# Attention and two MoE layers on one core: conversions of the first weights moved from three steps to the two behind them

## The chip, the cores and the metric

One Trainium2 chip, one of its cores. The metric is the device time of the kernel in microseconds (us), from one launch of the whole program. Lower is better.

## What is computed

The reference chains three layers over 4 batches of 576 tokens:

```python
scores = np.where(causal, -1e9, q @ k.T / 8 + cum_i - cum_j)     # 8 heads of 64
attn = softmax(scores) @ v                                       # -> x, 2304 x 512
h = np.maximum(np.maximum(x @ w1, x @ w2), x @ w3)               # 512 -> 768
x2 = h @ w_out                                                   # 768 -> 512
h = x2 @ w_in                                                    # 512 -> 2048
g = (a0 + a1*h + a2*h**2 + a3*h**3) / (1 + abs(b0)*abs(h) + abs(b1)*h**2 + 1e-6)
out = g @ w_out2                                                 # 2048 -> 512
```

All weights arrive as float64. The kernel converts them on the chip.

## The kernel before

**Stages.** Attention and the first MoE layer run interleaved (up to about 480 us of the profiled execution), the second MoE layer follows. A matrix product is made of three matmuls over parts called high and low: the value rounded for TensorE and what rounding left.

**Attention** goes by pairs of heads (class `Pair`, line 278) and by two groups of query rows: group 0 is rows 0 to 319, group 1 is rows 320 to 575. The first batch's eight pairs have one group each: pairs 0 to 3 do group 0, pairs 4 to 7 group 1. So the fourth pair, number 3, is the last one that group 0 of the first batch needs. A `Unit` (line 358) is one head of a pair's group, and there is one unit per step of the main loop (line 606). It is spread over three steps: in its own step the scores (TensorE, lines 388 to 391), masking and minimum (VectorE, line 392), the exponential (ScalarE, line 399) and the scaling by the row sums (GpSimd, line 412, or ScalarE, line 410); in the next step its transposes (line 432) and their copies (line 434); in the step after that, for every second unit, the product with v (`attend`, line 448), its high part x (ScalarE, line 455) and low part (VectorE, line 456). So the fourth pair's two units are those of steps 6 and 7, and its x is written in step 9.

**Idle matmuls.** For pairs 0 to 3, `exercised` (line 80) issues two matmuls of 512 columns on constant data ahead of each real group (line 84). Nothing reads them.

**First MoE layer.** `moe1_units` (line 517) gives 22 units for each batch and group: 18 of `moe1_h` (line 475, twelve matmuls on lines 482 to 484, one weight tile per unit, taken in the order in which tiles are converted) and four of `moe1_o` (line 499), which need all tiles of the second weights. The first 22 come into a queue in step 9. `fill` (line 565) is called six times a step; it pops conversions as `conv_due` (line 587) wants, and spreads the 22 units over the steps up to 24.

**Conversions.** There are 18 of 512 elements a partition (the first weights, `convert_w1`, line 214), then 12 of 256 (`convert_wo`, line 223). Each has four stages (`stages`, line 169): `magnitude` on ScalarE (line 181), `bits` as four instructions on VectorE (lines 186, 187, 188, 191), `high` on ScalarE (line 197), `low` on GpSimd (line 200). Raw weights are loaded by SyncE's queue (`load_raw`, line 163, 512 KB for each of the first 18) into six buffers, three ahead at the start and then two ahead of the conversion (`pipelined`, line 249). Two conversions are made before the loop. Then:

```python
def conv_due(step):
    state["c"] += 0.15 if step < 7 else 0.5
    return NCONV - int(state["c"])
```

which, at six calls a step, is 0.9 a step up to step 6 (eight conversions in all by then) and three a step from step 7 on, 30 by step 14.

**Order of the work.** The program is traced in this order, and the Tile scheduler then orders each engine's instructions: earlier in the program means higher priority, and an instruction of lower priority goes ahead when, by the scheduler's own model of time, nothing of higher priority is ready. Engines then execute in that fixed order. `tc.issue_after(ins)` keeps what its block traces behind `ins` on the engine of `ins`; on line 398 the exponentials of the first batch's units are so kept behind the last x. `keep_in_program_order` pins the order of the raw loads.

Of the kernel before, what the change touches and what calls it, by code (L numbers as in the profile page):

```python
# [8 lines left out]
F32 = mybir.dt.float32  # L9
F32R = mybir.dt.float32r  # L10
I32 = mybir.dt.int32
AF = mybir.ActivationFunctionType
# [25 lines left out]
def kernel(  # L38
    ctx: ExitStack, tc: tile.TileContext, q, k, v, f, w1, w2, w3, w_out, m2_in, m2_out, m2_a, m2_b, out
):  # L40
    nc = tc.nc
# [8 lines left out]
    NPAIR = H // 2  # L50
    NB = len(Q0)

    def r32(ap):
        return ap.bitcast(F32)
# [25 lines left out]
    def exercised(bank, n):  # L80

        if n < 4:
            for _ in range(WARM):
                nc.tensor.matmul(bank, warm[:, 0], wide, start=True, stop=True)
        return bank
# [36 lines left out]
    LOOK, WHOLE, PRE = 2, 6, 2  # L122
# [36 lines left out]
    E_LO, E_HI = 2.0**-15, float.fromhex("0x1.dffffep+16")  # L159

    raws = {}

    def load_raw(src, nm_):
        shape = list(src.shape)
        rp, rt, rb = (mpool, "x1", 8) if shape[1] * shape[2] <= 256 else (wpool, "x2", 6)
        raws[nm_] = rp.tile(shape[:-1] + [2 * shape[-1]], I32, name=f"raw_{nm_}", tag=rt, bufs=rb)
        tc.keep_in_program_order(nc.sync.dma_start(raws[nm_], src.bitcast(I32)))

    def stages(split, src, nm_, pool, tag, bufs, pin):
        shape = list(src.shape)  # L170
        at = {}

        def held(ins):
            return tc.keep_in_program_order(ins) if pin else ins

        def magnitude():
            raw = raws.pop(nm_)
            raw = raw.rearrange("p c (f t) -> p c f t", t=2)
            at["low"], at["top"] = raw[:, :, :, 0], raw[:, :, :, 1]
            at["t"] = pool.tile(shape, I32, name=f"cv_{nm_}", tag=tag, bufs=bufs)  # L180
            held(nc.scalar.activation(at["t"].bitcast(F32), at["top"].bitcast(F32), AF.Abs))

        def bits():
            t, low, top = at["t"], at["low"], at["top"]
            tf = t.bitcast(F32)
            held(nc.vector.tensor_scalar(tf, tf, E_LO, E_HI, op0=ALU.max, op1=ALU.min))
            nc.vector.tensor_scalar(t, t, 0x07FFFFFF, 3, op0=ALU.bitwise_and, op1=ALU.logical_shift_left)
            nc.vector.scalar_tensor_tensor(
                out=t, in0=low, scalar=29, in1=t, op0=ALU.logical_shift_right, op1=ALU.bitwise_or
            )  # L190
            nc.vector.scalar_tensor_tensor(
                out=t, in0=top, scalar=-0x40000000, in1=t, op0=ALU.bitwise_and, op1=ALU.bitwise_or
            )

        def high():
            at["hi"], at["lo"] = split()
            held(nc.scalar.activation(at["hi"], at["t"].bitcast(F32), AF.Copy))

        def low():
            held(nc.gpsimd.tensor_tensor(at["lo"], at["t"].bitcast(F32), r32(at["hi"]), op=ALU.subtract))  # L200

        return [magnitude, bits, high, low]

    def convert(hi, lo, src, nm_, pool, tag, bufs):
# [6 lines left out]
    def raw_w1(fc, j):  # L211
        return rows((w1, w2, w3)[j])[:, :, fc * P : (fc + 1) * P], f"w{j}_{fc}"

    def convert_w1(fc, j):
        if fc not in w1t:
            w1t[fc] = [wpool.tile([P, 3, NDC, P], F32R, name=f"w1{x}_{fc}", tag="w", bufs=12) for x in "hl"]
        hi, lo = (t[:, j] for t in w1t[fc])
        convert(hi, lo, *raw_w1(fc, j), mpool, "x1", 8)
# [30 lines left out]
    def pipelined(work, look, begun=False):  # L249

        n = len(work)

        def go(i):
            for j in range(0 if i == 0 and not begun else i + look + (i == 0), min(i + look + 1, n)):
                work[j][0]()
            work[i][1]()

        return [lambda i=i: go(i) for i in range(n)]
# [5 lines left out]
    def pinned(ld):  # L264
        tc.keep_in_program_order(ld)
# [92 lines left out]
    class Unit:  # L358
# [77 lines left out]
        def attend(self):  # L436

            p, h, g = self.pair, self.h, self.g
            if h == 0:
                return  # L440
            lo, hi = GQ[g]
            w = hi - lo
            ot = exercised(ps_o.tile([P, 512], F32, name=f"o_{self.nm}", tag="o"), p.n)
            order = list(GCH[g].items())
            with tc.high_priority():
                for j, (c, (col, q0)) in enumerate(order):
                    for i in (1, 0):
                        mm = nc.tensor.matmul(  # L448
                            ot[SIDES[i][0], q0 - lo : w], p.v[:, c, i], p.pt[g][:, i, col : col + hi - q0],
                            start=(j == 0), stop=(j == len(order) - 1),  # L450
                        )
                        if (j, i) != (0, 1):
                            pinned(mm)
            x = mpool.tile([P, 2, w], F32R, name=f"x_{self.nm}", tag=f"x{g}", bufs=(6, 8)[g])
            out_ = nc.scalar.activation(x[:, 0], ot[:, :w], AF.Copy)
            nc.vector.tensor_tensor(x[:, 1], ot[:, :w], r32(x[:, 0]), op=ALU.subtract)  # L456
            xt[p.b, p.hp, g] = x
            if p.b == 0:
                last["x"] = out_.ins


    hs = {}
# [54 lines left out]
    def moe1_units(b, g):  # L517
        return [lambda fc=fc, j=j: moe1_h(b, g, fc, j) for fc in range(NF1) for j in range(3)] + [
            lambda dc=dc: moe1_o(b, g, dc) for dc in range(NDC)
        ]  # L520
# [7 lines left out]
    conv = [  # L528
        (lambda fc=fc, j=j: load_raw(*raw_w1(fc, j)), lambda fc=fc, j=j: convert_w1(fc, j))
        for fc in range(NF1)  # L530
        for j in range(3)
    ]
# [2 lines left out]
        for fc in range(NF1)  # L535
        for z in range(2)
    ]
    ahead = [load_ for load_, _ in conv[: LOOK + 1]]
    conv = pipelined(conv, LOOK, True)
    wps = [(c, z) for c in range(NF2) for z in range(2)]  # L540
    conv2 = []
    for i, cz in enumerate(wps):
# [12 lines left out]
    for n, p in enumerate(pairs):  # L555
        if p.hp == NPAIR - 1:
            at = first.get(n + 1, len(slots)) + 1
# [4 lines left out]
    state = {"m": 0, "of": 1, "n": 0}  # L562
# [22 lines left out]
    state["c"] = state["c2"] = 0.0  # L585

    def conv_due(step):
        state["c"] += 0.15 if step < 7 else 0.5
        return NCONV - int(state["c"])

    pairs[0].load()
# [14 lines left out]
    for step in range(len(slots) + 2):  # L606
        u = slots[step] if step < len(slots) else None
        t = slots[step - 1] if 0 <= step - 1 < len(slots) else None
        o = slots[step - 2] if 0 <= step - 2 < len(slots) else None
        prep, NPRE = [], 0  # L610
        if u is not None and u.pair.n + 1 < len(pairs):
            n = u.pair.n + 1
            at = first[n] - (2 if len(pairs[n - 1].groups) == 2 else PRE if pairs[n].whole else 1)
            if step == at:
                prep = pairs[n].prepare()
                NPRE = pairs[n].ng + 1
        if o:
            o.attend()
            if step in ready:
                queue.append((step, [x for bg in ready[step] for x in moe1_units(*bg)]))  # L620
        if step == 16:
            pinned(nc.sync.dma_start(ab[:, 0:4], m2_a.partition_broadcast(P)))
            pinned(nc.sync.dma_start(ab[:, 4:6], m2_b.partition_broadcast(P)))
        fill(step)
        if t:
            t.turn(0)
        fill(step)
        if t:
            for bank in range(1, len(GBANK[t.g])):
                t.turn(bank)  # L630
        fill(step)
        for f_ in prep[:NPRE]:
            f_()
        if u:
            blks = GBLK[u.g]
            u.begin()
            for i in blks[:-1]:
                u.scores(i)
            fill(step)
            u.scores(blks[-1])  # L640
        else:
            fill(step)
        fill(step)
        for f_ in prep[NPRE:]:
            f_()
        fill(step)
        if u:
            u.normalise()
        for p in lvat.get(step, []):
            p.load_v()  # L650
        if prep and n + 1 < len(pairs):
            pairs[n + 1].load()
# [50 lines left out]
    a0, a1, a2, a3, b0, _, b1, one = (ab[:, i : i + 1] for i in range(8))  # L703
# [161 lines left out]
```

## Time and profile before

| | |
|---|---|
| median of 3 runs | 956.12 us (954.08 to 957.19) |
| the profiled execution's own time | 953.65 us |
| its span, first to last instruction | 951.6 us |
| TensorE's mean granted share of full clock | 0.996 |
| busy: TensorE, VectorE, ScalarE, GpSimd | 98%, 76%, 68%, 25% |
| chain that ended last: TensorE, VectorE, ScalarE, issue, DMA | 84%, 9%, 2%, 2%, 2% |

The busy share of TensorE counts modelled ends of matmuls that overlap in the pipeline; distances between starts tell more. The chain follows the last instruction back to what released each step, so its shares say which engine set the end.

### The profile page before, as it was taken

The page shows a single profiled execution, that of the slowest core. Times are in us where ns is not written, and L with a number is a line of the kernel's source. Part 1 is how long each engine was busy: PE and PEld are TensorE (multiplying, and loading weights), DVE is VectorE, ACT ScalarE, POOL GpSimd, SP SyncE. Part 2 cuts the span into 40 slices and gives each one's busy share as a digit, 9 for nine tenths or more (in the row PEclk, how much of TensorE's full clock was granted, in tenths as well). Part 3 has the DMA queues.
Part 4 walks back from the last instruction along what each step waited for, and adds up shares of the span by engine and source line. Part 5 has one row for each costly group of instructions (what it writes and reads, how often), then busy time and mean ns, then how long its engine had stood idle before and what let it go on. Part 6 is the DMA issues. An engine that isn't in the chain of part 4 may idle for free.

```text
span 951.6 us, 16833 instructions
## 1 busy us (share of the span) xinstructions
PE 930.5 (98%) x5780; PEld 825.3 (87%) x5780; DVE 723.0 (76%) x1692; ACT 648.8 (68%) x1542; POOL 241.3 (25%) x392
## 2 busy tenths in 40 slices
PE   6999999999999999999999999999999999999998
PEld 4758989988999989999999988888888888899997
DVE  8897854556776767534296969888888988899996
ACT  6898877767767676646354567667666766677765
POOL 4654424444555555414132300000000000000000
PEclk9989999999999999999999999999999999999999
DMA  7871431133556455220246386011002102100000
GB/s 192 227 229 52 111 106 45 44 87 102 149 151 194 124 159 165 65 79 2 68 145 192 118 296 235 1 45 45 0 1 70 42 1 67 44 1 1 34 1 34
DMA packets 125741, 88.52 MB, mean 93 GB/s; under 512 B 74572, under 2 KB 110424, under 8 KB 125656
## 3 DMA queue, kind: packets, MB, share of 16 engines
q1 hardware_dynamic: 125656, 87.45, 30.7%
q8 instruction: 46, 0.75, 0.3%
q14 instruction: 39, 0.32, 0.1%
HBM read 64.73 MB, written 22.69 MB: 92 GB/s over the span
## 4 chain that ended last, share of the span: by engine, by line
PE 84%; DVE 9%; ACT 2%; issue 2%; DMA 2%; SPq 1%; POOL 0%; ACTq 0%; DVEq 0%; POOLq 0%
PE hq L740 7%; PE oo L788 7%; PE hq L738 7%; PE hq L739 7%; PE oo L789 7%; PE oo L787 7%; PE h L482 6%; PE h L483 6%; PE h L484 6%; PE o L448 5%; PE tp L432 5%; PE x2p L508 2%; PE s L391 2%; PE s L390 2%; PE x2p L510 2%
## 5 line engine op out<-in xcount | busy, mean ns | idle before, releaser
L482 PE MATMUL h<-x,w1h 128*128 128x320 f32 (+1 forms) x576 | 175.7, 305 | 2.3 <-DVE x L456 2.0
L483 PE MATMUL h<-x,w1h 128*128 128x320 f32 (+1 forms) x576 | 172.2, 299 | 0.0
L484 PE MATMUL h<-x,w1l 128*128 128x320 f32 (+1 forms) x576 | 171.8, 299 | 0.0
L482 PEld LDWEIGHTS h<-x,w1h 128*128 128x128 f32 x576 | 109.2, 190 | 4.3 <-DVE x L456 2.3
L788 PE MATMUL oo<-wp,gh 128*128 128x512 f32 x288 | 112.7, 391 | 0.0
L399 ACT ACTIVATE e<-e,st 128x64 f32<-128x64 f32 (+4 forms) x160 | 89.0, 557 | 34.2 <-DVE st L392 33.0
L787 PE MATMUL oo<-wp,gh 128*128 128x512 f32 x288 | 112.1, 389 | 0.0
L747 ACT ACTIVATE s<-hq 128x512 f32<-128x512 f32 (+1 forms) x80 | 44.3, 554 | 97.6 <-PE hq L740 97.5
L483 PEld LDWEIGHTS h<-x,w1h 128*128 128x128 f32 x576 | 109.4, 190 | 0.4 <-issue 0.2
L484 PEld LDWEIGHTS h<-x,w1l 128*128 128x128 f32 x576 | 109.2, 190 | 0.0
L789 PE MATMUL oo<-wp,gl 128*128 128x512 f32 x288 | 109.2, 392 | 0.0
L412 POOL TENSOR_SCALAR e<-e,rs 128x64 f32<-128x64 f32 (+4 forms) x144 | 79.0, 563 | 103.3 <-DVE rs L406 87.8
L392 DVE CUSTOM_DVE_ANT_0 e<-s,mask 128x320 f32<-128x320 f32 (+3 forms) x160 | 67.0, 431 | 38.9 <-PE s L391 33.3
L750 DVE SCALAR_TENSOR_TENSOR s<-s,ab,u 128x512 f32<-128x512 f32 (+1 forms) x80 | 55.7, 697 | 32.3 <-ACT u L748 32.1
L434 ACT ACTIVATE pt<-tp 128x384 f32<-128x384 f32 (+3 forms) x160 | 69.4, 469 | 15.7 <-PE tp L432 14.0
L432 PE MATMUL tp<-ident,e 128*128 128x128 f32 (+1 forms) x480 | 75.8, 276 | 1.3 <-POOL e L412 0.9
L740 PE MATMUL hq<-x,wil 128*128 128x512 f32 (+1 forms) x192 | 69.9, 364 | 0.0
L738 PE MATMUL hq<-x,wih 128*128 128x512 f32 (+1 forms) x192 | 69.8, 364 | 0.0
L739 PE MATMUL hq<-x,wih 128*128 128x512 f32 (+1 forms) x192 | 69.7, 363 | 0.0
L789 PEld LDWEIGHTS oo<-wp,gl 128*128 128x128 f32 x288 | 54.1, 188 | 11.3
L787 PEld LDWEIGHTS oo<-wp,gh 128*128 128x128 f32 x288 | 54.1, 188 | 10.4
L788 PEld LDWEIGHTS oo<-wp,gh 128*128 128x128 f32 x288 | 54.1, 188 | 10.4
(133 smaller groups left out, 2433.3 us busy)
## 6 DMA issues: line engine op xcount, KB each, us to landing
raw_w<-in_moe_w_dram SPq DMA_DIRECT2D x18, 512.0 KB
raw_wp<-in_moe_w_out_dram SPq DMA_DIRECT2D x32, 256.0 KB
wpd<-wp SPq DMA_DIRECT2D x32, 256.0 KB
raw_wi<-in_moe_w_in_dram SPq DMA_DIRECT2D x32, 256.0 KB
wp<-wpd SPq DMA_DIRECT2D x10, 768.0 KB
x2d<-xo SPq DMA_DIRECT2D x16, 320.0 KB
out_dram<-ob SPq DMA_DIRECT2D x18, 256.0 KB
kn<-in_k_dram SPq DMA_DIRECT2D x32, 128.0 KB
```

What stands on the lines that cost most here:

```text
L399: nc.scalar.activation(e[:nr], e[:nr], AF.Exp, bias=m, scale=-1.0, accum_out=l)
L412: nc.gpsimd.tensor_scalar(e, e, self.rs[:, 1, j : j + 1], 0.0, op0=ALU.mult, op1=ALU.add)
L432: nc.tensor.transpose(tp[:kr, dst : dst + P], self.e[i][:, Q0[c] : Q1[c]], ident)
L482: nc.tensor.matmul(hp_[:, :w], wh[:, j, dc], xs[dc][:, 1], start=(dc == NDC - 1), stop=False)
L483: nc.tensor.matmul(hp_[:, :w], wh[:, j, dc], xs[dc][:, 0], start=False, stop=False)
L484: nc.tensor.matmul(hp_[:, :w], wl[:, j, dc], xs[dc][:, 0], start=False, stop=(dc == 0))
L738: nc.tensor.matmul(hp_[:, :w], wih[:, dc, fs], xh, start=(dc == 0), stop=False)
L739: nc.tensor.matmul(hp_[:, :w], wih[:, dc, fs], xl, start=False, stop=False)
L740: nc.tensor.matmul(hp_[:, :w], wil[:, dc, fs], xh, start=False, stop=(dc == NDC - 1))
L787: nc.tensor.matmul(o, g[0][:, ts_], wh_, start=(fc == 0), stop=False)
L788: nc.tensor.matmul(o, g[0][:, ts_], wl_, start=False, stop=False)
L789: nc.tensor.matmul(o, g[1][:, ts_], wh_, start=False, stop=(fc == NF2 - 1))
```

## The change

After the eighth conversion none is due in steps 7, 8 and 9. One raw load is issued at the head of each of these three steps instead. In steps 10 and 11 conversions come at one per `fill`, six a step, then three a step as before; the 30th falls in step 15. From the ninth on, raw weights are loaded five ahead instead of two. Every conversion traced from step 10 on has its first ScalarE instruction kept behind the fourth pair's x.

```diff
     raws = {}
+    fourth = {"x": None}
...
-            held(nc.scalar.activation(at["t"].bitcast(F32), at["top"].bitcast(F32), AF.Abs))
+            with tc.issue_after(fourth["x"]) if fourth["x"] else nullcontext():
+                held(nc.scalar.activation(at["t"].bitcast(F32), at["top"].bitcast(F32), AF.Abs))
...
                 last["x"] = out_.ins
+                fourth["x"] = fourth["x"] or (out_.ins if p.n == NPAIR - 1 else None)
...
-    ahead = [load_ for load_, _ in conv[: LOOK + 1]]
-    conv = pipelined(conv, LOOK, True)
+    loads = [load_ for load_, _ in conv]
+    ahead = [loads.pop(0) for _ in range(LOOK + 1)]
+
+    def convert_next(i, run):
+        while loads and NC - len(loads) < i + (LOOK if i < HELD else FAR) + 1:
+            loads.pop(0)()
+        run()
+
+    NC, HELD, FAR = len(conv), 8, 5
+    conv = [lambda i=i, run=run: convert_next(i, run) for i, (_, run) in enumerate(conv)]
...
-        state["c"] += 0.15 if step < 7 else 0.5
+        state["c"] += 0.15 if step < 7 else 0.0 if step < 10 else 1.0 if step < 12 else 0.5
...
+        if 7 <= step < 10:
+            loads.pop(0)()
         if o:
             o.attend()
```

## Rows read from the trace of the kernel before

**Rows 1.** Stretches: busy us of each engine (xcount), granted clock, DMA share, GB/s.
```profile
30.90:50.90 20.00, 20.00 (x121) 15.68 (x120) 16.12 (x44) 16.84 (x50) 10.53 (x13) 1.00 0.90 245
50.80:74.20 23.40, 19.23 (x86) 11.52 (x84) 23.40 (x53) 21.24 (x54) 13.70 (x13) 0.85 0.65 193
74.20:142.50 68.30, 67.30 (x483) 62.67 (x483) 47.48 (x145) 53.99 (x140) 26.96 (x41) 1.00 0.34 91
200.00:480.00 280.00, 277.75 (x2162) 258.36 (x2161) 170.52 (x555) 182.60 (x543) 125.80 (x222) 1.00 0.40 115
```
**Rows 2.** The chain that ended last, in order of time: start us, us, what.
```profile
41.81 1.34 PE o L448 x12
...
46.83 0.47 PE s L84 x2
47.30 0.54 PE s L388 x2
47.84 0.33 PE tp L432 x3
...
70.57 1.68 DVE cv_w L188
...
73.79 0.41 DVE x L456
...
142.47 2.17 PE o L448 x20
```
**Rows 3.** TensorE in order of time: start us, us, instruction, count, idle before.
```profile
61.23 1.02 PE L388 MATMUL s<-kf,qf 66*128 66x448 f32 x2 [1.18 <-DVE st L392]
...
66.40 2.62 PE L448 MATMUL o<-pt,v 128*64 128x320 f32 x12
...
74.24 0.42 PE L482 MATMUL h<-x,w1h 128*128 128x320 f32 x1 [2.04 <-DVE x L456]
...
76.10 0.31 PE L482 MATMUL h<-x,w1h 128*128 128x320 f32 x1
```
**Rows 4.** VectorE's groups, 50.8 to 74.3 us: busy us, mean ns, idle before.
```profile
L188 DVE SCALAR_TENSOR_TENSOR cv_w<-raw_w,cv_w 128x512 int32<-128x512 int32 x8 | 7.4, 927 | 0.0
...
L392 DVE CUSTOM_DVE_ANT_0 e<-s,mask 128x320 f32<-128x320 f32 (+3 forms) x7 | 3.2, 460 | 0.0
```
**Rows 5.** TensorE's groups, same stretch and columns.
```profile
L388 PE MATMUL s<-kf,qf 66*128 66x320 f32 (+2 forms) x18 | 8.2, 551 | 2.0 <-DVE st L392 2.0
L432 PE MATMUL tp<-ident,e 128*128 128x128 f32 (+1 forms) x21 | 4.2, 312 | 0.2
L448 PE MATMUL o<-pt,v 128*64 128x320 f32 (+2 forms) x24 | 4.0, 489 | 0.0
```
**Rows 6.** ScalarE's groups, same stretch and columns.
```profile
L197 ACT ACTIVATE w1h<-cv_w 128x512 fp32r<-128x512 f32 x7 | 4.4, 625 | 0.0
L181 ACT ACTIVATE cv_w<-raw_w 128x512 f32<-128x512 f32 x6 | 4.0, 666 | 0.0
```
**Rows 7.** VectorE's group of first weights left behind 74.3 us, to 142.5 us.
```profile
L191 DVE SCALAR_TENSOR_TENSOR cv_w<-raw_w,cv_w 128x512 int32<-128x512 int32 x1 | 0.7, 677 | 0.0
```
**Rows 8.** VectorE in order of time: start us, us, instruction.
```profile
63.76 1.38 DVE L187 TENSOR_SCALAR cv_w<-cv_w 128x512 int32<-128x512 int32 x1
65.06 1.49 DVE L186 TENSOR_SCALAR cv_w<-cv_w 128x512 f32<-128x512 f32 x1
...
67.48 0.41 DVE L186 TENSOR_SCALAR cv_w<-cv_w 128x512 f32<-128x512 f32 x1
```
**Rows 9.** GpSimd in order of time, same columns.
```profile
63.58 2.67 POOL L200 TENSOR_TENSOR w1l<-cv_w,w1h 128x512 fp32r<-128x512 f32 x2
```
**Rows 10.** SyncE's queue in order of time.
```profile
54.39 3.86 SPq L167 DMA_DIRECT2D raw_w<-in_moe_w_dram  x4
58.34 8.27 SPq L167 DMA_DIRECT2D raw_wo<-in_moe_w_out_dram  x4
69.06 0.38 SPq L269 DMA_DIRECT2D v<-in_v_dram  x1
```

## The prediction

> **What bounds the kernel now.** I first read busy time by stretches [rows 1]. From 200 to 480 us TensorE is busy for 277.75 of 280 us, so behind the start nothing but TensorE's own work sets the pace: what TensorE loses early is lost at the end, and what it gains early stays, unless it is lost again later. The stretch that is different is 50.8 to 74.2 us, steps 7 to 9. There VectorE is busy for all of its 23.4 us, TensorE's granted clock is 0.85 on average, and TensorE has 86 matmul records, where the 20 us before had 121 [rows 1].
>
> Next I read the chain [rows 2]. Up to about 50 us it runs over TensorE. Then it runs over VectorE's conversion lines, such as the 1.68 us piece of line 188 at 70.57, and it comes back to TensorE only through the fourth pair's low part of x (line 456 at 73.79). In TensorE's own order of time [rows 3] the same is seen from the other side: a score matmul waits 1.18 us for VectorE at 61.23, the fourth pair's product with v takes 2.62 us at 66.40, where the same twelve matmuls took 1.34 at 41.81 [rows 2], and the first matmul of the MoE layer starts at 74.24 after 2.04 us of waiting for x. The doubled time is the clock: a mean of 0.85 over the stretch [rows 1] is (1 - 0.85) x 23.4 / 0.5 = 7.0 us at the lower of two levels, 1.2 GHz instead of 2.4. What came before the fall was TensorE waiting for VectorE [rows 3].
>
> **What the change removes.** The unions of VectorE's time: of the 23.4 us, masking and minimum (lines 392), x and the reciprocals take about 6.3 us (the largest group, 3.2 us, in [rows 4]). The other 17.1 us are conversions of the first weights, about 7.5 of them (eight instructions of line 188 [rows 4], seven of others), so 2.3 us each. All of these leave the stretch. Eight conversions are allowed before the fourth pair's x, and the kernel before has, behind 74.3 us, only one last instruction of line 191 left of eighteen conversions [rows 7]. So some 9.3 conversions move behind x: the 7.5 of this stretch and about two that had been pulled ahead of it. The new order on ScalarE makes this certain, since VectorE's four instructions need line 181's result.
>
> What TensorE must do in the stretch, at full clock: 18 score matmuls at 0.54 / 2 = 0.27 us [rows 2, 5], 4.9 us; 21 transposes at 0.33 / 3 = 0.11, 2.3 us; 24 products with v at 1.34 / 12 = 0.11, 2.7 us. The other 23 of the 86 are idle matmuls (0.47 / 2 = 0.235 each [rows 2]) and transposes of keys and queries, about half each; at 0.17 they make 3.9 us. Together 13.8 us, so the stretch holds **23.4 - 13.8 = 9.6 us** that a free VectorE could give back, the clock's part included.
>
> Not all of it comes back. ScalarE's 21.24 us there [rows 1] lose 4.4 + 4.0 us of conversions [rows 6] and so about 12.8 remain, below TensorE's 13.8; but steps 8 and 9 hold scores without idle matmuls, and a chain of score, minimum, exponential and transpose has waits of its own. The row nearest is the 20 us before, where TensorE never sat idle beside 0.9 conversions a step [rows 1]: nothing lost. At the other end, the waits and the lower clock stay as they are in the last part, some 4 us. I take 1.1 us, nearer to the first, since VectorE, which ended those waits, is three quarters freed. First term: **-8.5 us** (-9.6 to -5.6).
>
> **What it adds behind x.** From 74.2 to 142.5 us, where pair 7's product with v starts [rows 2], whose x lets the next 22 units begin, VectorE is busy for 47.48 of 68.3 us and ScalarE for 53.99 [rows 1]. Into this come 9.3 conversions. On ScalarE they cost 0.625 + 0.666 = 1.29 us each [rows 6], 12.0 us against 14.3 idle. On VectorE at 2.3 us they cost 21.4 us against 20.8 idle. So both engines would be full, which no chain of dependent instructions reaches. What covers TensorE is the store of MoE units: twelve matmuls, 76.10 - 74.24 = 1.86 us each [rows 3]; the eight that have weights are 15 us of work, and a conversion each 2.3 us adds the next. What gives way is the attention of steps 10 to 17, whose masks queue on VectorE behind the conversions and whose transposes and products wait for them, and the last four units, for which the twelve second conversions are due one step later.
>
> Bounds of this second term: nothing, if the 12 second conversions slip behind pair 7's x and the units cover the rest; or +13 us, if the lost attention runs alone (rival D). A packing of about 94% fits the work of 47.5 + 21.4 = 68.9 us into 73 us, which against 68.3 is 5 us late, with part of it covered by units that run meanwhile. I take **+4 us**, between nothing and the full lateness, nearer to the latter.
>
> A GpSimd instruction beside a conversion can stretch it: lines 187 and 186 took 1.38 and 1.49 us while two subtractions of line 200 ran from 63.58 to 66.25, and 0.41 us at 67.48 alone [rows 8, 9]. My 2.3 us is a mean that holds such meetings. The Trainium skill, SBUF — State Buffer, section "Who interferes with whom", states that VectorE and GpSimd share a port pair as an exclusive lock, held for a whole instruction, and that the later one blocks. By that rule one subtraction met in full per conversion would make the sum about 9 us longer and the gain would be gone; the trace agrees so far that two instructions stretched to more than three times 0.41 us beside line 200.
>
> **Moved DMAs.** Three raw loads issue in steps 7 to 9 instead of nine; SyncE's queue had sat 3.86 and 8.27 us in raw loads before pair 4's v at 69.06 [rows 10], so this stretch loses work, and x waited for VectorE and no load [rows 2]: nothing either way. Behind x, loads five ahead fill all six buffers: each next load waits for a conversion to end, and keys, queries and v of pairs 5 to 7 queue behind it on SyncE. They are due a step or two later, some 9 us a step (142.5 - 66.4 over eight steps), and a wait for one conversion is 2.3 us: nothing, or 2 to 3 us if one meets an idle TensorE. GpSimd's 9.3 subtractions (half of 2.67 us each [rows 9], 12 us) fit beside its 26.96 of 68.3 [rows 1]. The three added issues cost no engine anything.
>
> **Sum.** -8.5 + 4 = -4.5 us. Against the profiled execution, 953.65 - 4.5 = 949.2; that execution lies 2.5 below the median of 956.12, and on the median the forecast is **951.6 us**. A difference under 0.3% (2.9 us, about the spread of the three runs) cannot be told from none.
>
> **The rivals.**
> - **A, forecast:** x comes 8 us sooner, about half is given back. 951.6. Chance 0.38.
> - **B, nearly all is kept:** the scheduler lets units cover TensorE and second conversions slip behind pair 7's x. For it: units are taken in the order of the conversions, and from 200 us VectorE has room, 170.52 of 280 us [rows 1]. Against: ScalarE and VectorE are both over 95% loaded by the sums above. 956.1 - 8 = 948. Chance 0.20.
> - **C, the bound only moves:** VectorE is the bound in steps 10 to 12 instead, because packed conversions meet line 200 more often. One more meeting costs 1.49 - 0.41 = 1.1 us [rows 8]; in six of the 9.3 it is 6.5 us more than summed, of which some 4 us reach the end. Then 951.6 + 4 = about 955.5. Chance 0.27.
> - **D, slower:** the scheduler's fixed order puts the conversions of steps 10 and 11 in one block on VectorE; the units are used up during it, and the attention of steps 13 to 17 runs alone. ScalarE without conversions has some 44 us for eight steps (53.99 less 10 [rows 1]), 5.4 a step; TensorE has about 3.6, so five steps leave 9 us idle, and a fall of the clock like that of steps 7 to 9 adds 3.5 (half of 7.0). 12.5 - 8.5 = 4 slower, 960. It decides from the point where TensorE loses more than the 8.5 us regained. Against it: units alone are 33 us of cover. Chance 0.15.
>
> **How the numbers follow.** Faster is A and B, 0.58; same is C, 0.27; slower is D, 0.15. The range reaches from the full 9.6 kept and half a us of spread, 946.0, to C with the spread of runs, 957.5; D lies mostly outside.
>
> **What would show it.** Right: no stretch of clock 0.5 near 62 us; the first line 482 at 63 to 67 us instead of 74.24; VectorE under half busy between 51 and 63 us and nearly full for the 30 us behind; line 448 of pair 7 some 4 us earlier than 142.5. Wrong: line 482 still starts after 70 us (another wait held x), or line 448 of pair 7 comes at 142 us or later (all given back), or line 482 stands waiting on weights of line 200 or 197.

## The result and the profile after

The changed kernel takes 961.94 us (median of 6 runs, 960.38 to 962.78) against 955.8 for the kernel before in the same job: ratio 1.0058, 95% interval 1.0044 to 1.0071. It is 6 us slower where 4.5 us less were forecast, and lies above the forecast's range of 946.0 to 957.5. The profiled execution took 961.48 us with a span of 959.7, against 953.65 and 951.6.

Line numbers of the changed kernel are two or three higher: scores 390 to 393, masks 394, transposes 434, product with v 450, x 457 and 458, MoE matmuls 485 to 487, maximum 493; conversions 183 and 199 (ScalarE), 188 to 190 and 193 (VectorE), 202 (GpSimd).

Stretches of the changed kernel, columns as in [rows 1]:

```profile
50.80:64.20 13.40, 13.14 (x79) 9.04 (x77) 5.43 (x21) 10.40 (x31) 2.47 (x6) 1.00 0.31 85
50.80:74.20 23.40, 22.05 (x127) 16.21 (x126) 14.71 (x43) 18.28 (x49) 4.31 (x7) 1.00 0.29 79
64.20:94.20 30.00, 26.62 (x171) 22.59 (x171) 29.14 (x60) 26.61 (x62) 14.50 (x13) 1.00 0.50 147
74.20:142.50 68.30, 59.35 (x400) 51.55 (x399) 61.26 (x141) 52.51 (x129) 34.55 (x39) 0.98 0.38 111
124.00:130.60 6.60, 4.92 (x31) 3.67 (x31) 6.38 (x18) 2.98 (x8) 2.46 (x4) 1.00 0.00 0
130.60:134.00 3.40, 3.40 (x18) 1.95 (x20) 3.40 (x10) 2.19 (x6) 1.69 (x3) 0.50 0.02 5
200.00:480.00 280.00, 277.74 (x2168) 257.38 (x2165) 168.77 (x551) 184.34 (x547) 126.39 (x223) 1.00 0.39 114
```

Against [rows 1], the stretch from 50.8 to 74.2 us has what was forecast: 127 matmul records instead of 86, clock 1.00 instead of 0.85, VectorE busy for 14.71 us instead of all of it. The one behind has lost: from 74.2 to 142.5 us TensorE has 400 records instead of 483 and is busy for 59.35 us instead of 67.30, while VectorE rose from 47.48 to 61.26. VectorE is nearly full in the 30 us behind x, as forecast (29.14 us). From 200 us on both kernels are alike. The clock's lower level, 1.2 GHz, has gone from near 62 us and stands at 130.6 to 134.0, behind a stretch in which TensorE was busy for only 4.92 of 6.60 us.

TensorE of the changed kernel in order of time, columns as in [rows 3]:

```profile
64.20 0.41 PE L485 MATMUL h<-x,w1h 128*128 128x320 f32 x1 [0.22 <-DVE x L458]
...
93.65 0.42 PE L485 MATMUL h<-x,w1h 128*128 128x320 f32 x1 [1.25 <-DVE m L493]
...
98.07 0.41 PE L485 MATMUL h<-x,w1h 128*128 128x320 f32 x1 [2.39 <-DVE m L493]
...
149.01 2.17 PE L450 MATMUL o<-pt,v 128*64 128x256 f32 x20
```

The MoE layer begins at 64.20 us instead of 74.24 [rows 3]: a lead of 10.0 us. Pair 7's product with v comes at 149.01 instead of 142.47 [rows 2], 6.5 us behind. So 16.5 us go between those two points. The two rows in the middle say how: a MoE unit, meant to be TensorE's cover, waits until VectorE's maximum has taken off the product of an earlier unit.

The chain that ended last, changed kernel, columns as in [rows 2]:

```profile
56.88 0.55 PE s L390 x2
...
63.19 0.44 ACT x L457
...
65.78 0.69 DVE cv_w L190
...
93.59 1.75 DVE cv_w L193
...
106.93 0.60 DVE cv_w L190
...
126.03 0.74 DVE cv_wo L188
...
130.49 3.88 PE o L450 x20
```

Before, the chain came back to TensorE behind VectorE's piece at 73.79 us [rows 2]. Of the 66.2 us between 64.2 and 130.4 its pieces now give VectorE 34.0, ScalarE 15.5, issue 8.5 and TensorE only 6.1; behind that, TensorE's next piece is the one at 130.49.

VectorE's groups of the first weights in the changed kernel, 64.2 to 142.5 us, columns as in [rows 4]:

```profile
L193 DVE SCALAR_TENSOR_TENSOR cv_w<-raw_w,cv_w 128x512 int32<-128x512 int32 x10 | 11.2, 1132 | 0.1
...
L190 DVE SCALAR_TENSOR_TENSOR cv_w<-raw_w,cv_w 128x512 int32<-128x512 int32 x10 | 6.8, 681 | 0.0
L189 DVE TENSOR_SCALAR cv_w<-cv_w 128x512 int32<-128x512 int32 x10 | 6.7, 679 | 0.1
...
L188 DVE TENSOR_SCALAR cv_w<-cv_w 128x512 f32<-128x512 f32 x10 | 5.1, 523 | 0.7 <-ACT cv_w L183 0.7
```

The three groups that belong to line 188 of [rows 4], kernel before, 50.8 to 74.2 us:

```profile
L191 DVE SCALAR_TENSOR_TENSOR cv_w<-raw_w,cv_w 128x512 int32<-128x512 int32 x7 | 5.8, 826 | 0.0
L187 DVE TENSOR_SCALAR cv_w<-cv_w 128x512 int32<-128x512 int32 x8 | 5.4, 670 | 0.0
L186 DVE TENSOR_SCALAR cv_w<-cv_w 128x512 f32<-128x512 f32 x7 | 4.1, 585 | 0.0
```

Ten conversions moved behind x. The four means make 1132 + 681 + 679 + 523 = 3.02 us a conversion after and 927 + 826 + 670 + 585 = 3.01 before. Instructions overlap a little; counted from what the one before left to its own end, a conversion held VectorE for 2.75 us after (27.5 for ten) and 2.76 before (20.0 for 29 instructions). So a conversion did not become dearer by being moved. The forecast's 2.3 us was too low from the start. The twelve second conversions, counted likewise, grew from 17.8 to 21.8 us.

### The profile page after: what moved, and what is told of

It is laid out like the page before. It is cut to its first block, busy times and chain, and to the rows that moved or that the text cites. A ratio compares the mean times of both kernels' runs of the same rounds, so it can differ in the third digit from the quotient of the medians.

```text
span 959.7 us, 16850 instructions
## 1 busy us (share of the span) xinstructions
PE 931.8 (97%) x5780; PEld 823.8 (86%) x5780; DVE 728.6 (76%) x1692; ACT 648.3 (68%) x1542; POOL 242.1 (25%) x392
## 4 chain that ended last, share of the span: by engine, by line
PE 79%; DVE 10%; ACT 5%; issue 2%; DMA 2%; POOL 1%; SPq 0%; ACTq 0%; DVEq 0%; POOLq 0%
PE hq L753 7%; PE hq L751 7%; PE oo L802 7%; PE oo L801 7%; PE hq L752 7%; PE oo L800 7%; PE h L485 5%; PE h L486 5%; PE h L487 5%; PE o L450 5%; PE tp L434 5%; PE x2p L511 2%; PE s L393 2%; PE s L392 2%; PE x2p L513 2%
## 5 line engine op out<-in xcount | busy, mean ns | idle before, releaser
L414 POOL TENSOR_SCALAR e<-e,rs 128x64 f32<-128x64 f32 (+4 forms) x144 | 76.3, 544 | 107.1 <-DVE rs L408 88.9
L752 PE MATMUL hq<-x,wih 128*128 128x512 f32 (+1 forms) x192 | 69.7, 363 | 0.0
```

The source lines that it names most:

```text
L414: nc.gpsimd.tensor_scalar(e, e, self.rs[:, 1, j : j + 1], 0.0, op0=ALU.mult, op1=ALU.add)
L752: nc.tensor.matmul(hp_[:, :w], wih[:, dc, fs], xl, start=False, stop=False)
```

## The experiments

Each run has its median and its ratio to the kernel before in its own job (955.8 to 957.1 us). "Shift" is (ratio - 1) x 956 us; the change has +5.5. Unless said otherwise the edit is to the changed kernel.

**1. The loads alone.** Raw weights five ahead; no rest, no doubling, no hold.

```diff
-            with tc.issue_after(fourth["x"]) if fourth["x"] else nullcontext():
+            if True:
-        state["c"] += 0.15 if step < 7 else 0.0 if step < 10 else 1.0 if step < 12 else 0.5
+        state["c"] += 0.15 if step < 7 else 0.5
```

> The changed kernel without its rest, its two doubled steps and its hold behind the fourth pair's x: conversions are due as before, and only the raw loads run further ahead. Load theory (VectorE's conversions between the fourth pair's x and pair 7's x set the loss): as before, 954.5 to 957.5 us. Rival, the loads (SyncE's queue or the buffers filled five ahead cost the time): 958 us or more.

957.2 us, 1.0009 [0.9999, 1.0019]. The loads cost nothing that can be measured, with the conversions where they were.

**2. The rest without the two doubled steps.**

```diff
-        ... 0.0 if step < 10 else 1.0 if step < 12 else 0.5
+        ... 0.0 if step < 10 else 0.5
```

> The changed kernel with three conversions a step from step 10 on instead of six in steps 10 and 11. Load theory: VectorE still has ten more first-weight conversions behind x, only the last few second ones slip later, so a part of the loss remains: 955 to 959 us, with VectorE busy over 90% from 64 to 125 us. Rival, the bunching (the doubled steps alone cost the time): the rest's 8 to 10 us are kept, 946 to 950 us.

962.24 us, 1.006 [1.0043, 1.0076]. Equally slow: the doubled pace alone is not the cause. TensorE here also waits for converted weights that come later at this pace, 5.2 us in all from 64 to 147 us, which it does not in the changed kernel.

**3. VectorE's share of the ten mostly out.** Three of their four VectorE instructions are left out; ScalarE's and GpSimd's stay.

```diff
+    LIGHT = [f"w{i % 3}_{i // 3}" for i in range(8, 18)]
...
+            if nm_ in LIGHT:
+                return
```

> The changed kernel; the ten first-weight conversions behind the fourth pair's x leave out three of their four VectorE instructions (the bits of the mantissa are not put together), everything else stays. Load theory: some 23 us of VectorE's time go, VectorE is no longer full, the lead of 10 us at the fourth pair's x is kept: 945 to 950 us. Rivals (loads, hold on ScalarE, order): 958 us or more.

960.25 us, 1.0036 [1.002, 1.0051]. Only 2 us back. The profiled execution was the fastest of ten, 956.66 us. The stretch behind x in it, columns as in [rows 1]:

```profile
64.20:142.50 78.30, 71.07 (x481) 63.75 (x481) 54.80 (x144) 64.44 (x160) 35.96 (x46) 0.98 0.43 120
```

TensorE's longest wait in this run, 64 to 147 us (what waits, for what: us in total, times, longest us; line numbers are three higher than in the changed kernel):

```profile
PE s L395 <- DVE q1s L330: 4.7, 2, 3.7
```

VectorE is busy for 54.80 of 78.3 us, TensorE still for only 71.07. Freeing VectorE alone is not enough. Ahead of that wait the chain of this run goes over SyncE's queue, columns as in [rows 2]:

```profile
86.73 1.85 SPq L169
...
91.85 3.54 DMA kn<-in_k_dram
```

From 85.76 to 95.39 us it is the queue, where raw loads (line 169 there) stand between loads for later pairs, and then the loading of keys. With VectorE freed, the loads were the next limit there.

**4. The low parts of all 22 conversions as memsets.** GpSimd's subtractions are left out for the ten and for the twelve second ones (low parts zero).

```diff
+    LATE = [f"w{i % 3}_{i // 3}" for i in range(8, 18)] + [f"wo_{i // 2}_{i % 2}" for i in range(12)]
...
         def low():
+            if nm_ in LATE:
+                nc.gpsimd.memset(r32(at["lo"]), 0.0)
+                return
```

> The changed kernel; the 22 conversions behind the fourth pair's x write zeros for the low part with a GpSimd memset, which reads nothing, in place of the subtraction on GpSimd. Meetings of GpSimd and VectorE stretch VectorE's conversion instructions by some 16 us in sum between 64 and 135 us. If these meetings are on the path: 950 to 955 us, and instructions of VectorE near their shortest times. If the load without them is what counts: 958 to 962 us.

951.56 us, 0.9942 [0.9922, 0.9963]: shift -5.5, so 11 us below the change. GpSimd's subtractions, for which the forecast had no term of their own, are the largest single item found.

**5. Second conversions allowed to slip.**

```diff
-        ... 1.0 if step < 12 else 0.5
+        ... 1.0 if step < 12 else 0.2
```

> The changed kernel, but from step 12 on conversions are due at 1.2 a step instead of three, so that the second weights end in step 20 and not in step 15. Load theory (both VectorE and ScalarE are full between the fourth pair's x and pair 7's x, so work that can wait must wait): some eight second conversions, 1.8 us of VectorE each, leave that stretch, pair 7's x comes 8 to 12 us sooner than in the changed kernel: 950 to 956 us. Rival (the loss is made before, by the first weights alone in steps 10 and 11): 959 to 962 us.

972.7 us, 1.0165 [1.0146, 1.0184]. TensorE of this run in order of time:

```profile
169.22 0.39 PE L511 MATMUL x2p<-hh,wo 128*128 128x320 f32 x1
...
180.72 0.28 PE L485 MATMUL h<-x,w1h 128*128 128x256 f32 x1
```

The last units of the first 22 (line 511) are still running at 169 us, and the next 22 start at 180.72 (before: 146.3). Second conversions have no slack to give.

**6. The subtraction on VectorE**, so that GpSimd reads nothing beside it; **7.** the same in the kernel before.

```diff
+            eng = nc.vector if nm_ in LATE else nc.gpsimd
-            held(nc.gpsimd.tensor_tensor(at["lo"], ...
+            held(eng.tensor_tensor(at["lo"], ...
```

> The changed kernel with the subtraction of the 22 conversions behind the fourth pair's x on VectorE instead of GpSimd: 0.4 to 0.7 us more of VectorE's work for each, no meeting of GpSimd's subtraction with it. Meeting theory (a meeting costs VectorE about a microsecond, and GpSimd's queue holds up the keys and queries of pairs 6 and 7): 952 to 957 us. Load theory (only the sum of VectorE's work counts): no gain, 960 to 965 us.

959.9 us, 1.0029 [1.0016, 1.0041].

> The kernel before with the same 22 subtractions on VectorE. If the meetings cost time in the kernel before too: 951 to 954.5 us. If VectorE's added work in the full stretch of 51 to 74 us counts more: 957 to 960 us.

955.77 us, 0.9999 [0.9983, 1.0015]. In the changed kernel 2.7 us come back although VectorE does 22 instructions more; in the kernel before nothing changes.

**8. The ten conversions left out**, zeros by GpSimd memsets that wait for nothing.

```diff
+        if nm_ in GONE:
+            raws.pop(nm_)
+            for x_ in (hi, lo):
+                nc.gpsimd.memset(r32(x_), 0.0)
+            return
```

> The changed kernel; the ten first-weight conversions behind the fourth pair's x are left out (both parts of these weights are zeros, written by GpSimd memsets), their raw loads stay. Load theory: the lead of 10 us is kept whole or nearly: 944 to 949 us, pair 7's x some 10 us before that of the kernel before. Rival (loads, order of units and attention, the second weights' conversions): 954 us or more.

952.15 us, 0.9945 [0.9928, 0.9962]. A poor test: the memsets went too early into GpSimd's queue, the fourth pair's x came at 69.7 us instead of 63.2, and most of the lead was lost. Run 13 mends this.

**9. ScalarE's share alone.** Of the ten only the two ScalarE instructions stay.

```diff
+        def only_scalar():
+            ...
+            for x_ in split():
+                with tc.issue_after(fourth["x"]):
+                    nc.scalar.activation(x_, top, AF.Abs)
...
+        return [only_scalar] if nm_ in GONE else [magnitude, bits, high, low]
```

> The changed kernel; of the ten first-weight conversions behind the fourth pair's x only ScalarE's part stays (two instructions behind the hold, which write the rounded raw words to both parts); VectorE's and GpSimd's parts are left out. Load theory (VectorE's time behind x, meetings with GpSimd included, eats the lead): the fourth pair's x at 63 to 64 us, pair 7's x at 135 to 140 us, 946 to 951 us. Rival (ScalarE's part and the hold are enough to lose it): pair 7's x at 147 us or later, 956 us or more.

961.67 us, 1.0058 [1.0036, 1.0079]. The first 20 us behind x in this run, columns as in [rows 1]:

```profile
64.20:84.20 20.00, 16.10 (x84) 13.17 (x85) 5.59 (x18) 19.90 (x44) 0.86 (x1) 0.91 0.43 135
```

Not a clean test either: with nothing between them, the twenty instructions ran in one burst on ScalarE (19.90 of 20 us), and pair 4's x came at 93.1 us instead of 84.5. It shows that a burst on ScalarE can cost as much, and leaves open what the paced share costs; run 18 bounds that.

**10. The subtraction without its wait for ScalarE.** GpSimd subtracts the value from itself: same size, same engine, low parts zero.

```diff
+            other = at["t"].bitcast(F32) if nm_ in LATE else r32(at["hi"])
```

> The changed kernel; the 22 subtractions behind x take a value from itself, so that GpSimd no longer waits for ScalarE's rounding, while reads, writes and time stay the same (the low parts come out as zeros). With the memset in their place the kernel took 951.6 us. If the meetings with VectorE made that difference: 958 to 963 us, as the changed kernel. If GpSimd's waits for ScalarE in its queue made it: 950 to 954 us.

957.34 us, 1.0011 [0.9999, 1.0024]. 4.5 us back with GpSimd reading as much as ever. GpSimd's waits, 64 to 152 us, columns as in run 3, in the changed kernel and then in this run:

```profile
POOL w1l L202 <- ACT w1h L199: 17.9, 3, 12.9
POOL wo L202 <- ACT wo L199: 17.2, 9, 5.7
...
POOL w1l L204 <- DVE cv_w L194: 19.0, 4, 10.2
POOL wo L204 <- DVE cv_wo L194: 8.9, 7, 4.0
```

The run does not take the waiting away: the subtractions now waited for VectorE's last instruction instead, 27.9 us against 35.1. What did change is that VectorE's conversions held it for 5.4 us less (table below). So it does not show that waiting in GpSimd's queue has a price.

**11. and 12. Fewer conversions moved:** some 1.5 and 2 a step in steps 7 to 9, then three, without the loads in these steps.

```diff
-        ... 0.0 if step < 10 else 1.0 if step < 12 else 0.5
+        ... 0.25 if step < 10 else 0.5
```

> The changed kernel with half a rest: 1.5 conversions a step in steps 7 to 9, then three a step, and no loads of their own in these steps. Load theory: about half the lead, 4 to 6 us at the fourth pair's x, and half the conversions moved, 12 us of VectorE's time against 21 idle, so most of the lead is kept: 951 to 955 us. Rival (any shift past x gives back what it gains, by the order of units and attention): 956 to 960 us.

957.36 us, 1.0005 [0.999, 1.002].

> The same with two conversions a step in steps 7 to 9: three of the nine moved. Load theory: a lead of 3 us at the fourth pair's x, nearly all kept: 952 to 955 us. Rival: 956 to 959 us.

957.33 us, 1.0008 [0.9994, 1.0022] (0.34 in place of 0.25). x of the fourth pair came at 65.0 and 66.5 us, 6.3 and 4.8 sooner than before, and the end did not move: what is gained there is paid back behind, at both doses.

**13. The ten left out and held.** Zeros are made by two GpSimd instructions that read the fourth pair's x, so that they can't run early.

```diff
+        if nm_ in GONE:
+            raws.pop(nm_)
+            x3 = r32(xt[0, NPAIR - 1, 0] ...
+            for x_ in (hi, lo):
+                ... nc.gpsimd.tensor_scalar(to, x3, 0.0, 0.0, op0=ALU.mult, op1=ALU.add)
+            return
```

> The changed kernel; the ten first-weight conversions behind the fourth pair's x are left out: both parts are zeros that two GpSimd instructions make from the fourth pair's x, so that they can't come before it. If the conversions' work is what eats the lead: the fourth pair's x at 64 us, pair 7's x at 134 to 138 us, 944 to 950 us. If the lead can't be kept in any case (units and attention do not fill TensorE that early): 955 us or more.

946.98 us, 0.9904 [0.9886, 0.9922]. The stretch behind x in this run, same columns:

```profile
64.20:142.50 78.30, 77.75 (x559) 71.25 (x560) 49.50 (x160) 62.02 (x165) 39.37 (x66) 1.00 0.40 103
```

TensorE is busy for 77.75 of 78.3 us. The lead of 10.0 us is worth 9.2 at the end if the conversions are not paid for; the ten conversions cost 14.7 (from -9.2 to +5.5), counted without what the twenty instructions that stand in for them may cost. Some 3 us of this lie in TensorE's clock, whose mean granted share over some 960 us was 0.9995 in this run's four executions and 0.9963 in the changed kernel's six; whether that comes from the waits that are gone or from the values that differ, no run separates.

**14. Raw weights two ahead, no loads in the steps** (against a burst of five conversions right behind x).

```diff
-    NC, HELD, FAR = len(conv), 8, 5
+    NC, HELD, FAR = len(conv), 8, 2
...
-        if 7 <= step < 10:
-            loads.pop(0)()
```

> The changed kernel without the three raw loads in the rest and with raw weights two ahead instead of five, so that two or three conversions and not five start at once at the fourth pair's x. If the burst counts: 954 to 958 us. If not: 960 to 964 us.

960.54 us, 1.0046 [1.003, 1.0062]. About 1 us back, within the two intervals' overlap: the burst is a small matter at most.

**15. ScalarE's share of the ten out.** VectorE reads the raw words, held behind the low part of x, and makes the high part in place of one of its four; GpSimd's subtraction stays and waits for VectorE instead of ScalarE.

```diff
+            if nm_ in GONE:
+                return
...
+            if nm_ in GONE:
+                nc.vector.tensor_scalar(at["hi"], tf, E_LO, E_HI, op0=ALU.max, op1=ALU.min)
+                return
```

> The changed kernel; of the ten conversions ScalarE's two instructions are left out (VectorE reads the raw words and writes the rounded part itself, still four instructions, held behind the low part of the fourth pair's x; GpSimd's subtraction stays; sign and range are not what they were). If ScalarE's share of 13 us is what fills the way: 950 to 955 us. If VectorE's and GpSimd's queues are: 958 to 964 us.

961.67 us, 1.0059 [1.0039, 1.0079]. Nothing back, though ScalarE fell to 50.63 us in the stretch behind x of this run (same columns):

```profile
64.20:142.50 78.30, 69.01 (x464) 61.72 (x462) 69.15 (x163) 50.63 (x131) 36.59 (x40) 0.98 0.39 111
```

**16. The kernel before with run 4's memsets.**

> The kernel before with the memset in place of the 22 later subtractions (their low parts are zeros). If GpSimd's reads cost time in the kernel before as well: 949 to 953 us, and the gain seen with the changed kernel is none of the change's. If they matter only when conversions are packed behind x: 955 to 957 us.

955.32 us, 0.9992 [0.9978, 1.0006] (edit as in run 4). The same subtractions cost the kernel before nothing that can be measured. Why is read from this run's profile in the last section.

**17. Memsets for the ten alone**; the second conversions stay whole.

```diff
+    LATE = [f"w{i % 3}_{i // 3}" for i in range(8, 18)]
```

> The ten moved conversions keep their two ScalarE and four VectorE instructions; only their ten subtractions on GpSimd become memsets (low parts zero). The twelve second conversions stay whole. Meeting theory (what the moved conversions cost is mainly GpSimd's ten subtractions of two operands met by VectorE's packed conversions): at most 955, most of the 10 us that all 22 memsets gave. Queue theory (VectorE's and ScalarE's in-order work of the ten is the price, the subtractions add little): 958 or more. If the twelve second subtractions were the larger part of those 10 us: also 958 or more, with x of the fifth and sixth pair as late as in the changed kernel (114 and 134 us).

954.89 us, 0.9971 [0.996, 0.9983]: shift -2.8, 8.3 us below the change. The profiled execution was the slowest of ten, 957.79 us; line numbers are one higher than in the changed kernel. VectorE's groups of the first weights in this run, 64.2 to 142.5 us, columns as in [rows 4]:

```profile
L194 DVE SCALAR_TENSOR_TENSOR cv_w<-raw_w,cv_w 128x512 int32<-128x512 int32 x10 | 8.2, 834 | 0.1
L191 DVE SCALAR_TENSOR_TENSOR cv_w<-raw_w,cv_w 128x512 int32<-128x512 int32 x10 | 7.0, 705 | 0.0
...
L190 DVE TENSOR_SCALAR cv_w<-cv_w 128x512 int32<-128x512 int32 x10 | 4.6, 464 | 0.1
...
L189 DVE TENSOR_SCALAR cv_w<-cv_w 128x512 f32<-128x512 f32 x10 | 4.1, 422 | 1.5 <-ACT cv_w L184 1.5
```

Two of these instructions in order of time, columns as in [rows 8]:

```profile
77.00 1.29 DVE L194 SCALAR_TENSOR_TENSOR cv_w<-raw_w,cv_w 128x512 int32<-128x512 int32 x2
```

A conversion's four means are 2.43 us instead of 3.02. In the changed kernel, VectorE in order of time:

```profile
71.09 1.51 DVE L189 TENSOR_SCALAR cv_w<-cv_w 128x512 int32<-128x512 int32 x1
...
76.60 2.98 DVE L193 SCALAR_TENSOR_TENSOR cv_w<-raw_w,cv_w 128x512 int32<-128x512 int32 x2
```

What GpSimd did there in the changed kernel, same columns:

```profile
70.47 1.84 POOL L202 TENSOR_TENSOR w1l<-cv_w,w1h 128x512 fp32r<-128x512 f32 x1 [12.87 <-ACT w1h L199]
76.06 2.98 POOL L202 TENSOR_TENSOR w1l<-cv_w,w1h 128x512 fp32r<-128x512 f32 x2 [3.74 <-ACT w1h L199]
```

Two instructions that take 1.29 us alone took 2.98 beside two subtractions. One by one, the two end at 77.88 and 79.59 us, and the two subtractions at 77.33 and 79.03: each of VectorE's ends some 0.55 us behind the subtraction that it met.

The first subtraction waited 12.87 us for ScalarE at the head of GpSimd's queue, but nothing behind it came late by that: the first low part of a unit's output started at 79.14 us, 0.07 behind ScalarE's copy (in this run, without the subtractions, at 79.56). From 64 to 140 us of the changed kernel GpSimd's other instructions (lines 316, 330 and 499) start at most 0.7 us after the instruction of ScalarE that feeds them. In the kernel before the longest such delay is 2.4 us. So the 8.3 us are read as time that the subtractions take from VectorE, not as time that GpSimd's queue stood.

**18. VectorE's share alone.** As run 15, and with memsets for the ten low parts.

```diff
+            if nm_ in GONE:
+                nc.gpsimd.memset(r32(at["lo"]), 0.0)
+                return
```

> The ten moved conversions keep only VectorE's four instructions each, held behind the low part of the fourth pair's x; ScalarE's two and GpSimd's subtraction are out (low parts are memsets). Queue theory (VectorE's block of forty in-order instructions alone keeps masks, maxima and key shifts waiting): 955 or more, fifth pair's x at 110 us or later. Meeting theory (they cost much only where GpSimd reads beside them): at most 951, fifth pair's x before 105 us, an instruction of 512 elements near 0.41 to 0.7 us.

952.53 us, 0.9955 [0.9942, 0.9969]: shift -4.3, between the two expectations. The x of pair 5, which the expectation calls the fifth, came at 105.1 us (113.7 in the changed kernel), just outside the second expectation; the time lies 1.5 us above it. The stretch behind x in this run, columns as in [rows 1]:

```profile
64.20:142.50 78.30, 75.21 (x526) 67.20 (x526) 68.65 (x192) 58.95 (x160) 27.36 (x44) 1.00 0.45 126
```

**What the runs say together.** Taken away one behind the other, the ten conversions' 14.7 us are: the subtractions 8.3 (run 17), ScalarE's two instructions 1.5 (run 18; the intervals of 17 and 18 overlap, so it may be nothing), VectorE's four 4.9 (run 13); each is good to about 2 us by the intervals. The order matters: taken away alone, VectorE's part gave 2 us (run 3) and ScalarE's nothing (run 15), while the subtractions were still there.

Where GpSimd's part was changed, the time followed the time that VectorE spent on conversions behind x (49.3 us in the changed kernel, counted in the profiled execution from what the one before left, subtractions on VectorE included):

```
run                        VectorE's conversions   less than change   time less than change
17 ten as memsets                  40.7                  8.6                 8.3
4  22 as memsets                   37.0                 12.3                11.0
18 VectorE's part alone            38.9                 10.3                 9.8
10 no wait for ScalarE             43.9                  5.4                 4.5
6  subtraction on VectorE          46.3                  2.9                 2.7
```

In runs 2, 14, 15 and 3 it did not: they had 3.9, 5.1, 2.1 and 20.7 us less on VectorE and 0 to 2 us less time. So VectorE's total is not the only limit. In run 2 TensorE waited for the weights, and in run 3 the chain shows loads in SyncE's queue; for runs 14 and 15 it stays open. Each kernel is also ordered anew by the scheduler, so a difference of 1 or 2 us between runs may be its order and not the edit.

None of the kernels that compute every conversion is faster than the kernel before; the forms that tie with it are runs 1, 7, 11 and 12.

## Why the prediction was wrong

**First term, -8.5: right.** The lead is 10.0 us at the first MoE matmul, 0.4 above the ceiling of 9.6, and run 13 keeps 9.2 of it. The clock no longer falls near 62 us, the first MoE matmul falls in the forecast's 63 to 67, and VectorE is 41% busy from 50.8 to 64.2 (5.43 of 13.4).

**Second term, +4: this step failed.** It is 14.7 by the runs, and 16.5 between the two points of the profiles. Three of its sentences are to blame.

*"GpSimd's 9.3 subtractions ... fit beside its 26.96 of 68.3."* GpSimd did have room for them (busy for 34.55 of 68.3 us after), but the price fell on VectorE: 8.3 us, by holding its instructions (2.98 us for a pair instead of 1.29). The forecast knew of such meetings and took its 2.3 us as a mean that holds them; that mean was too low.

*"On VectorE at 2.3 us they cost 21.4 us."* Ten at 2.75 are 27.5. The 2.3 came from what 6.3 us for other work had left over, and of that other work the trace has only some 4.5. With the second conversions' 4.0 us more, VectorE had 47.5 + 27.5 + 4.0 = 79 us to do where 68.9 were summed, and from x on there are 78.3 to 142.5. So VectorE was the bound again, only longer: rival C's case, at a much higher price. A packing of 94% was laid on a sum that was 10 us short. The 8.3 us of the subtractions are a part of this sum and do not come on top of it. With 79 us the forecast's own packing gives 84, from 64.2 to 148.2, and pair 7's product with v came at 149.0: the method was near, and what failed is the price of a conversion on VectorE, and that the second ones would lengthen too.

*"What covers TensorE is the store of MoE units."* A unit needs VectorE for its maximum and ScalarE and GpSimd for its copies. TensorE's waits in the changed kernel, 64 to 147 us:

```profile
PE h L485 <- DVE m L493: 4.1, 3, 2.4
PE h L485 <- ACT m L491: 1.4, 3, 0.8
```

The units themselves waited for the engines whose lateness they were to cover. Rival B's hope, that second conversions slip, is refuted by run 5.

**The rule on the port pair.** The forecast gave +9 us by the Trainium skill, SBUF — State Buffer, section "Who interferes with whom", and let its own term stand at the mean. By that rule whichever of the two comes first holds the shared ports for its whole instruction and the other one blocks; the pair at 76.60 us, whose two instructions each end some 0.55 us behind a subtraction, agrees, and the 8.3 us of run 17 are near the 9. In the kernel before the same subtractions cost nothing (run 16); the last section shows what took VectorE's place there.

**Moved DMAs: right as to size.** Run 1 puts the loads at nothing, with the conversions where they were. SyncE's queue did stand in raw loads behind x; the queue in the changed kernel, columns as in [rows 10]:

```profile
67.81 10.50 SPq L168 DMA_DIRECT2D raw_w<-in_moe_w_dram  x4
...
97.50 13.77 SPq L168 DMA_DIRECT2D raw_wo<-in_moe_w_out_dram  x5
```

But none of TensorE's waits above has a load as its releaser, and run 14, with two ahead, gives about 1 us. Only with VectorE freed, in run 3, did an idle TensorE meet the queue.

**The rivals.** D had the time (960) but not the mechanism: the units were not used up, since the eighteenth began at 120.0 and 120.1 us in the two kernels, and TensorE lost its time while they were there. Of its parts only the fall of the clock came, for 3.4 us (1.7 us lost). A sum that called both engines full already spoke for a loss, and the chance of 0.15 for one was too low.

## What to carry to other kernels

Before moving work behind a point, sum it on every engine that it touches, with each instruction at what it holds the engine in the crowded stretch, and ask of the cover whether it needs those same engines to finish. Room on one engine does not make free what is put there: here GpSimd had room, and VectorE's instructions paid. To find out whether a move can pay, leave the moved work out once, held at its place: here that gave 9.2 us to earn and 14.7 to pay in one run.

## What the hardware showed that was not expected

Two VectorE instructions of 1.29 us together took 2.98 beside two GpSimd subtractions that lasted as long: more than twice. A conversion is as long in the kernel before (3.01 us against 3.02), and yet leaving the 22 subtractions out gains nothing there (0.9992), while leaving out ten gives 8.3 us in the changed kernel. The profile of run 16 says what takes VectorE's place: its stretch from 50.8 to 74.2 us, columns as in [rows 1], and its chain, columns as in [rows 2].

```profile
50.80:74.20 23.40, 21.51 (x100) 13.06 (x98) 22.14 (x61) 22.73 (x58) 9.96 (x18) 0.85 0.72 204
```
```profile
56.00 5.30 DMA raw_w<-in_moe_w_dram
61.32 0.70 ACT cv_w L182
...
71.30 0.44 ACT x L459
```

ScalarE is now busy for 22.73 of 23.4 us (21.24 before), and from 50.9 to 71.7 us the chain is ScalarE for 15.2 us and one raw load for 5.3, and no longer VectorE. The fourth pair's x comes at the same 71.3 us. In that stretch ScalarE and the loads stood close behind VectorE; that they are the reason is read from this chain, and no run tests it.
